# Second layer's weights assembled during the first layer and parked in DRAM as float32

## The chip, the cores and the metric

The kernel runs on one NeuronCore of one Trainium2 chip. What counts is the device time of one launch in microseconds: median 1091.19 us of three runs (1089.95 to 1091.54). The profile shows one execution by itself; its own time was 1087.0 us.

## The reference, cut to what matters

Two attentions over the same q, k, v (4 batches, 8 heads, 576 positions, 64 wide), one on averages of four positions and one over the nearest seven positions, are added and reshaped to 2304 rows of 512. Two dense layers follow:

```python
h = x @ w_in                                   # 2304x512 @ 512x2048
g = np.where(h > 0, h, np.exp(np.minimum(h, 0)) - 1)
x = g @ w_out                                  # 2048 -> 512
gate = x @ w_gate                              # 512 -> 1536
val  = x @ w_val
out  = (gate / (1 + np.exp(-gate)) * val) @ w_o2   # 1536 -> 512, float32 out
```

The five weight matrices arrive as float64 (they are float32 draws times a float64 scalar). [...]

## The kernel before, in words

**Weights.** A weight "unit" is 128x1024 words of input (512 KB): two of the 128-wide blocks of the hidden dimension for a column matrix, one block of rows for an output matrix. The first layer has 32 units (16 "in", 16 "out"), the second 36 (12 each of "gate", "val", "o2"). `add_weights` makes a float32 unit from a raw one in four instructions: `size` (L339, ScalarE: a scaled copy of the high words), `words_a` (L343, VectorE: a shift), and `words_b` (L347 and L349, VectorE: sign bit, then the three top bits of the low word). `add_weight_split` then makes two fp32r parts from the float32 unit: a rounded copy (L275 on ScalarE or L277 on VectorE) and the remainder (L371, GpSimd: 128x512 subtract).

**Products.** A product of two split numbers is three matmuls (`products`, L659 to L661): high by high, high by low, low by high. The first layer goes over 8 chunks of 288 rows; chunk 0 uses whole float32 weights (L684, L689), the others the split ones. A step is one of the 16 hidden blocks f of a chunk: gemm1 (12 matmuls of 288 columns), Relu and Exp (L725, L733 ScalarE), a combination (L729 VectorE), a rounded copy `g` (L275 or L277), the remainder of g (L736 GpSimd), and gemm2 (12 matmuls). There are two banks for h, two buffers e and three buffers g. The second layer goes over 5 tiles of 512 rows (the last 256) with 12 steps of 36 matmuls each; sigmoid (L799), two multiplications (L802), a rounded copy (L804), a remainder (L805).

**Where weights live.** 33 places hold the split first-layer weights (32 used). A second-layer unit takes a place as soon as the last chunk has used its first-layer weight for the last time; three more places are in a pool of their own. So the split of the second layer's weights runs beside the last chunk of the first layer. This stretch, 16 steps long, is called **the change** below.

**What sets the order.** Every operation is a task with an engine, a modelled cost and a due time. `Work.run` plays the program through once when it is built, starts on each free engine the ready task with the lowest due time, and writes the instructions in that order. On the chip each engine goes through its list in order. Tasks of the first layer's chain have due times 14 earlier than their step. The attention of batches 1 to 3 is spread over the first layer's steps (`spans`).

**Memory in time.** Attention buffers are closed when the last rows are ready; `open_two` then opens the pools of raw weights, float32 units and x. The buffers of gated values (`y`, and every second `e`) are opened by `close_one`, after the first layer's last matmul and store; sigmoids of odd steps and all rounded copies of y wait for that.

Of the kernel before, what the change touches and what calls it, by code (L numbers as in the profile page):

```python
# [18 lines left out]
P = 128  # L19
# [208 lines left out]
def attention_moe_moe(ctx: ExitStack, tc: tile.TileContext, q, k, v, w_in, w_out, w_gate, w_val, w_o2, ident_in, mask_in, band_in, picks_in, out):  # L228
# [54 lines left out]

    work = Work()
    add = work.add
    w_slots = Places(lambda i: pools["w"].tile([P, 2, 512], F32R, tag=f"w{i}", name="w"), NW)
    w_slots.name = "w"

# [25 lines left out]


    BIAS = (1023 - 127) // 8
    wt, ww = {}, {}
    split_places = lambda: range(NW - 1, -1, -1)  # L320

    def load_w(key, t):
        kind, f = key
        if kind in ("in", "gate", "val"):
            src = {"in": w_in, "gate": w_gate, "val": w_val}[kind]
            nc.sync.dma_start(
                out=t.rearrange("p (k c) t -> p k (c t)", c=P),
                in_=src[:, 2 * f * P:2 * (f + 1) * P].rearrange("(k p) c -> p k c", p=P))
        else:
            src = {"out": w_out, "o2": w_o2}[kind]  # L330
            nc.sync.dma_start(out=t.rearrange("p c t -> p (c t)"), in_=src[f * P:(f + 1) * P, :])

    def pairs(t):
        return t.rearrange("p (c t) -> p c t", t=2)

    def add_weights(keys, dues, raws, whole, after=()):

        def size(w, r):
            nc.scalar.mul(w.t.bitcast(F32), r()[:, :, 1].bitcast(F32), 2.0 ** -BIAS)  # L339

        def words_a(w):
            t = w.t.bitcast(I32)
            nc.vector.tensor_scalar(out=t, in0=t, scalar1=3, scalar2=None, op0=ALU.logical_shift_left)  # L343

        def words_b(w, r):
            t = w.t.bitcast(I32)
            nc.vector.scalar_tensor_tensor(  # L347
                out=t, in0=r()[:, :, 1], scalar=-0x80000000, op0=ALU.bitwise_and, in1=t, op1=ALU.bitwise_or)
            nc.vector.scalar_tensor_tensor(  # L349
                out=t, in0=r()[:, :, 0], scalar=29, op0=ALU.logical_shift_right, in1=t, op1=ALU.bitwise_or)  # L350

        made = {}
        for n, key in enumerate(keys):
            due = dues[n]
            raw, w = raws(n), whole(n)
            room = [w.whole] if isinstance(w, Half) else []
            r = lambda raw=raw: pairs(raw.t.bitcast(I32).rearrange("p a b -> p (a b)"))
            add("sp", 0.5, due - 36.0, lambda key=key, r=r: load_w(key, r()), writes=[raw], nbytes=P * 4096, after=after)
            add("act", 0.69, due - 4, lambda w=w, r=r: size(w, r), reads=[raw, *room], writes=[w])
# [5 lines left out]
    def add_weight_split(key, due):  # L365

        u = ww[key]
        w = wt[key] = w_slots.new(split_places) if len(wt) < NW else w2_ring.new()
        add(COPIER, (0.6, 0.4), due - 2, lambda engine: copy(engine, w.t[:, 0], u.t.bitcast(F32)),
            reads=[u], writes=[w], second=0)  # L370
        add("pool", 1.3, due - 1, lambda: nc.gpsimd.tensor_tensor(  # L371
            out=w.t[:, 1], in0=u.t.bitcast(F32), in1=w.t[:, 0], op=ALU.subtract), reads=[u, w], writes=[w])


# [288 lines left out]
    def add_store(c, due, acc):  # L663
        x2d[c] = pools["dram"].tile([P, NP, T1], F32, tag=f"x2_{c}", name="x2d")
        stored[c] = []
        for i in range(NP):
            t = out_ring.new()
            add(COPIER, (0.5, 0.5), due - 1, lambda engine, c=c, i=i, t=t: copy(engine, t.t, acc[i].t[:, :T1]),
                reads=[acc[i]], writes=[t], second=0)
            stored[c].append(add("sp", 0.5, due, lambda c=c, i=i, t=t: nc.sync.dma_start(  # L670
                out=x2d[c][:, i], in_=t.t), reads=[t], nbytes=P * T1 * 4))

    def add_whole(f, due, acc, last):

        if f == 0:
            acc[0] = [bank(i) for i in range(NP)]
        h, e, g = bank(6, 7), e_ring.new(), g_ring.new()
        wi, wo, x = ww["in", f], ww["out", f], xt[0]
        ge = lambda: g.t[:, 0].bitcast(F32)

        def gemm1():
            begun.append(1)
            for i in range(NP):
# [9 lines left out]
        add_weight_split(("in", f), time1(NF1 + f))  # L693
# [5 lines left out]
        add_weight_split(("out", f), time1(NF1 + f + 1))  # L699
        if f == NF1 - 1:  # L700
            add_store(0, due, acc[0])

    def add_first():
        made = []
        acc, last = {}, {}
        for s, (c, f) in enumerate(order):
            due = time1(s)
            if c == 0:
                add_whole(f, due, acc, last)
                continue  # L710
            if f == 0:
                acc[c] = [bank(i) for i in range(NP)]
# [37 lines left out]

    x2r_ring = ring("f2", "x2r", [P, T2], 2, ordered=False)
    x2_ring = [ring("x" + "ab"[i], "x2", [P, 2, T2], 4, F32R) for i in range(2)]
    e2_ring = [ring("e2" + "ab"[i], "e2", [P, T2], 1) for i in range(2)]
    y_ring = ring("g2", "y", [P, 2, T2], 2, F32R)

    def add_second(opened, exps, first_done):
        x2t = {}
        for n, t0 in enumerate(range(0, N, T2)):
# [24 lines left out]
            for f in range(NF2):  # L783
# [3 lines left out]
                for kind, where in (("gate", (4, 5)), ("val", (6, 7))):  # L787
# [10 lines left out]
                e, y = e2_ring[f % 2].new(), y_ring.new()  # L798
# [5 lines left out]
                add("act", 0.6, due, lambda T=T, e=e, y=y: nc.scalar.copy(y.t[:, 0, :T], e.t[:, :T]), reads=[e], writes=[y], after=first_done)  # L804
# [20 lines left out]
    with tc.manual_schedule():  # L825
# [39 lines left out]
        for p in range(NP):  # L865
# [5 lines left out]
        words = add_weights(  # L871
            w1, w1_due, lambda n: w_slots.new(lambda: range(NW - 1, U1 - 1, -1)), lambda n: Half(whole[n // 2], n % 2))
# [25 lines left out]

        def close_one():
            one.close()  # L900
            for name in ("xb", "g2", "e2b"):
                open_pool(ctx, name, reuse_waits="tile")

        closed = [add("none", 0, 0, close_one, after=made)]
        r_ring = ring("r2", "r", [P, 512, 2], 3, I32)
        u_ring = ring("r2", "u", [P, 512], 3)
        w2_ring = ring("w2", "w", [P, 2, 512], len(w2) - NW, F32R)
        w2_due = [time2(f + (kind == "o2")) - 38.0 for kind, f in w2]
        add_weights(
            w2, w2_due, lambda n: r_ring.new(), lambda n: u_ring.new(), after=opened)  # L910
        wt.clear()
        for n, key in enumerate(w2):
            add_weight_split(key, w2_due[n])
        add_second(opened, exps, closed)
        work.run()

# [44 lines left out]
```

## Time and profile before

| | |
|---|---|
| median of 3 runs | 1091.19 us |
| profiled execution | 1087.0 us (span 1085.2 us) |
| TensorE busy | 1007.7 us of the span |
| VectorE / ScalarE / GpSimd busy | 553.4 / 396.9 / 326.1 us |
| mean granted TensorE clock | 0.959 |

The page cuts the span in 40 slices of 27 us. TensorE is at 9 tenths nearly throughout; the dips are in the first three slices (loading, attention of batch 0) and in slices 21 to 24 (543 to 651 us), where VectorE is at 8 to 9 tenths and the clock row falls to 8. Before that VectorE stands at 3 to 6 tenths, after it at 2.

Times in the trace are from the start of the span. A busy TensorE counts a matmul until its modelled end, so its rate is read from the distance between two starts.

### The profile page before, as it was taken

To read this page: it belongs to the slowest core of one execution; us is meant where nothing else is said; L and a number is where in the kernel's file an instruction comes from. 1 tells how busy PE (TensorE), PEld (TensorE's weight loads), DVE (VectorE), ACT (ScalarE), POOL (GpSimd) and SP (SyncE) were. 2 spreads that over 40 slices of the span, in tenths; PEclk is the share of its full clock that TensorE was granted. 3 is DMA by queue.
4 is the path that set the end of the run, shared out by engine and by line. 5 is a ranking of instruction groups with operands and counts; after the bars stand their busy time and mean duration, and the time that the engine had idled before them with its cause. 6 is when DMAs were issued, how large, how long until landed. Compare 5 with 4: busy or idle time off the path is not lost.

```text
span 1085.2 us, 18891 instructions
## 1 busy us (share of the span) xinstructions
PE 1007.7 (93%) x7540; PEld 878.3 (81%) x7540; DVE 553.4 (51%) x1003; ACT 396.9 (37%) x939; POOL 326.1 (30%) x355
## 2 busy tenths in 40 slices
PE   7669889999999999998987559999999999999998
PEld 5547679999999999998976548888888888888897
DVE  5899996553646446453389992222222222322232
ACT  4654555543554445453444442112112111211121
POOL 4473873452235222363466641001001000100000
PEclk8569999999999999999988989999999999999999
DMA  9958332131402111032055541002000100100010
GB/s 165 304 166 235 68 73 54 34 84 28 94 26 68 33 45 50 12 114 84 20 158 156 156 139 39 1 0 78 1 1 22 47 1 1 49 1 1 1 39 20
DMA packets 111335, 72.28 MB, mean 67 GB/s; under 512 B 71440, under 2 KB 105360, under 8 KB 111248
## 3 DMA queue, kind: packets, MB, share of 16 engines
q1 hardware_dynamic: 111104, 70.82, 24.0%
q8 instruction: 59, 0.97, 0.4%
q14 instruction: 28, 0.23, 0.1%
q10 hardware_dynamic: 144, 0.26, 0.1%
HBM read 61.62 MB, written 9.44 MB: 65 GB/s over the span
## 4 chain that ended last, share of the span: by engine, by line
PE 77%; DVE 11%; issue 4%; DMA 3%; POOL 2%; SPq 2%; ACT 1%; DVEq 0%; POOLq 0%; ACTq 0%
PE bank L659 24%; PE bank L661 23%; PE bank L660 23%; DVE u L347 3%; PE bank L526 1%; DVE u L349 1%; DVE u L343 1%; SPq L409 1%; DVE w L347 1%; PE bank L684 1%; DVE w L343 1%; PE bank L445 1%; DMA w<-in_v_dram 1%; POOL w L371 1%; PE bank L566 1%
## 5 line engine op out<-in xcount | busy, mean ns | idle before, releaser
L659 PE MATMUL bank<-x,w 128*128 128x288 f32 (+2 forms) x928 | 318.5, 343 | 23.4 <-DVE e L729 22.5
L660 PE MATMUL bank<-x,w 128*128 128x288 f32 (+2 forms) x928 | 312.4, 337 | 0.8 <-POOL x L647 0.8
L661 PE MATMUL bank<-x,w 128*128 128x288 f32 (+2 forms) x928 | 311.8, 336 | 0.0
L659 PEld LDWEIGHTS bank<-x,w 128*128 128x128 f32 x928 | 175.8, 189 | 46.1 <-DVE e L729 25.9
L802 DVE TENSOR_TENSOR e<-bank,e 128x512 f32<-128x512 f32 (+1 forms) x120 | 76.4, 637 | 251.2 <-ACT e L799 173.6
L660 PEld LDWEIGHTS bank<-x,w 128*128 128x128 f32 x928 | 176.8, 191 | 17.7 <-POOL x L647 1.1
L661 PEld LDWEIGHTS bank<-x,w 128*128 128x128 f32 x928 | 176.8, 191 | 16.2
L736 POOL TENSOR_TENSOR g<-e,g 128x288 fp32r<-128x288 f32 x112 | 97.6, 872 | 188.2 <-ACT g L275 147.6
L660 PE MATMUL bank<-g,w 128*128 128x288 f32 x448 | 134.6, 300 | 5.5 <-POOL g L736 5.5
L659 PE MATMUL bank<-g,w 128*128 128x288 f32 x448 | 136.7, 305 | 0.0
L661 PE MATMUL bank<-g,w 128*128 128x288 f32 x448 | 133.4, 298 | 0.0
L779 POOL TENSOR_TENSOR x<-x2r,x 128x512 fp32r<-128x512 f32 (+1 forms) x20 | 24.1, 1221 | 270.6 <-ACT x L778 270.6
L799 ACT ACTIVATE e<-bank 128x512 f32<-128x512 f32 (+1 forms) x60 | 33.4, 556 | 187.4 <-PE bank L661 186.4
L729 DVE SCALAR_TENSOR_TENSOR e<-e,bank 128x288 f32<-128x288 f32 x112 | 50.2, 448 | 100.8 <-ACT e L733 94.1
L659 PE MATMUL bank<-w,y 128*128 128x512 f32 x216 | 85.5, 396 | 10.3 <-ACT y L804 10.3
L660 PEld LDWEIGHTS bank<-g,w 128*128 128x128 f32 x448 | 86.3, 193 | 6.9 <-POOL g L736 6.8
L725 ACT ACTIVATE e<-bank 128x288 f32<-128x288 f32 x112 | 46.1, 412 | 119.7 <-PE bank L661 104.3
L804 ACT CAST y<-e 128x512 fp32r<-128x512 f32 (+1 forms) x60 | 34.7, 578 | 150.7 <-DVE e L802 133.3
L659 PEld LDWEIGHTS bank<-g,w 128*128 128x128 f32 x448 | 86.1, 192 | 2.8 <-issue 1.9
L661 PEld LDWEIGHTS bank<-g,w 128*128 128x128 f32 x448 | 86.2, 192 | 0.0
L661 PE MATMUL bank<-w,y 128*128 128x512 f32 x216 | 85.1, 394 | 0.2 <-DVE y L805 0.2
L660 PE MATMUL bank<-w,y 128*128 128x512 f32 x216 | 85.0, 394 | 0.0
(115 smaller groups left out, 1428.6 us busy)
## 6 DMA issues: line engine op xcount, KB each, us to landing
w<-in_moe_w_in_dram SPq DMA_DIRECT2D x16, 512.0 KB
w<-in_moe_w_out_dram SPq DMA_DIRECT2D x16, 512.0 KB
r<-in_moe_w_gate_dram SPq DMA_DIRECT2D x12, 512.0 KB
r<-in_moe_w_val_dram SPq DMA_DIRECT2D x12, 512.0 KB
r<-in_moe_w_out_dram SPq DMA_DIRECT2D x12, 512.0 KB
x2d<-o SPq DMA_DIRECT2D x32, 144.0 KB
out_dram<-x2r SPq DMA_DIRECT2D x17, 256.0 KB
vrows<-in_v_dram SPq DMA_DIRECT2D x66, 64.0 KB
```

The source lines that it names most:

```text
L343: nc.vector.tensor_scalar(out=t, in0=t, scalar1=3, scalar2=None, op0=ALU.logical_shift_left)
L347: nc.vector.scalar_tensor_tensor(out=t, in0=r()[:, :, 1], scalar=-0x80000000, op0=ALU.bitwise_and, in1=t, op1=ALU.bitwise_or)
L659: nc.tensor.matmul(ps, sh, mh, start=first, stop=False)
L660: nc.tensor.matmul(ps, sh, ml, start=False, stop=False)
L661: nc.tensor.matmul(ps, sl, mh, start=False, stop=last)
L725: nc.scalar.activation(e.t, h.t[:, :T1], AF.Relu, scale=-1.0)
L729: nc.vector.scalar_tensor_tensor(out=e.t, in0=e.t, scalar=-1.0, op0=ALU.add, in1=h.t[:, :T1], op1=ALU.max)
L736: add("pool", 0.82, due - URGENT, lambda e=e, g=g: nc.gpsimd.tensor_tensor(out=g.t[:, 1], in0=e.t, in1=g.t[:, 0], op=ALU.subtract), reads= ...
L779: add("pool", 1.3, due, lambda T=T, raw=raw, x=x: nc.gpsimd.tensor_tensor(out=x.t[:, 1, :T], in0=raw.t[:, :T], in1=x.t[:, 0, :T], op=ALU.s ...
L799: add("act", 0.6, due, lambda T=T, e=e, gate=gate: nc.scalar.activation(e.t[:, :T], gate.t[:, :T], AF.Sigmoid), reads=[gate], writes=[e], ...
L802: add("dve", 0.64, due, lambda T=T, e=e, x=x: nc.vector.tensor_tensor(out=e.t[:, :T], in0=x.t[:, :T], in1=e.t[:, :T], op=ALU.mult), reads= ...
L804: add("act", 0.6, due, lambda T=T, e=e, y=y: nc.scalar.copy(y.t[:, 0, :T], e.t[:, :T]), reads=[e], writes=[y], after=first_done)
```

## The change

Second-layer units are no longer assembled at the change. During chunks 1 to 6 each unit is loaded in two halves (128x512 words, 256 KB), assembled by the same four instructions on 256 columns, and the float32 half (128 KB) is stored to a DRAM tile. Two raw halves share the one spare weight place, two assembled halves a new tile `mid`. The first raw load waits for the last split of first-layer weights. At the change a unit is then loaded as float32 (256 KB, three buffers u) and only split. The first three units take the places of the extra pool, formerly the last three did. Also: pool of y and both e buffers are opened in `open_two`; sigmoids wait for the first layer's last Exp and rounded copies of y for nothing more; the attention of batches 2 and 3 is due 1 to 4 steps earlier; the last chunk's stores go through the five f buffers.

```diff
-    def add_weights(keys, dues, raws, whole, after=()):
...
+    def add_words(due, raw, u, reads=()):
...
+        part = 0.5 if isinstance(raw.room, Places) and raw.room is not w_raws else 1.0
+        add("act", 0.69 * part, due - 4, size, reads=[raw, *reads], writes=[u])
+        add("dve", 0.6 * part, due - 3, words_a, reads=[u], writes=[u])
+        return add("dve", 1.8 * part, due - 2.5, words_b, reads=[raw, u], writes=[u])
...
-            add("dve", 0.5, due - 3, lambda w=w: words_a(w), reads=[w], writes=[w])
-            made[key] = add("dve", 1.5, due - 2.5, lambda w=w, r=r: words_b(w, r), reads=[raw, w], writes=[w])
...
+    def add_weights_away(keys, dues, after):
+
+        spare = w_slots.new(lambda: range(NW))
+        raws = Places(lambda i: pairs(spare.t[:, i].bitcast(I32)), 2)
+        halves = Places(lambda i: mid[:, i], 2)
...
+            for i in range(2):
+                due = dues(2 * n + i)
+                raw, u = raws.new(lambda: range(2)), halves.new(lambda: range(2))
...
+                    nc.sync.dma_start(out=away[key][:, i * 256:(i + 1) * 256], in_=u.t)
...
+                add("sp", 0.5, due - 16.0, lambda key=key, raw=raw, i=i: load_w(key, raw.t, i), reads=[spare], writes=[raw],
+                    nbytes=P * 2048, after=after)
+                add_words(due, raw, u, [spare])
+                kept[key].append(add("sp", 0.5, due, store, reads=[u], nbytes=P * 1024))
...
-    e2_ring = [ring("e2" + "ab"[i], "e2", [P, T2], 1) for i in range(2)]
+    e2_ring = ring("e2", "e2", [P, T2], 2)
...
-                    reads=[gate], writes=[e], after=first_done if f % 2 else exps)
+                    reads=[gate], writes=[e], after=exps)
...
+        def w2_away(m):
+            return time1(2 * NF1) + (time1(6.9 * NF1) - time1(2 * NF1)) * m / (2 * len(w2))
...
-        spans = {1: (12, 24), 2: (42, 56), 3: (74, 88)}
+        spans = {1: (12, 24), 2: (41, 54), 3: (71, 84)}
...
-            for name in ("w2", "r2", "xa", "f2", "e2a"):
+            for name in ("w2", "r2", "xa", "f2", "e2", "g2"):
...
-        add_weights(
-            w2, w2_due, lambda n: r_ring.new(), lambda n: u_ring.new(), after=opened)
...
+            due = time2(f + (kind == "o2")) - 38.0
+            ww[key] = u = u_ring.new()
+            add("sp", 0.5, due - 8.0, lambda u=u, key=key: nc.sync.dma_start(out=u.t, in_=away[key]), writes=[u],
+                nbytes=P * 2048, after=[*opened, *kept[key]])
+            add_weight_split(key, due, w2_ring.new() if n < len(w2) - NW else w_slots.new(lambda: range(NW)))
```

The modelled VectorE cost of assembling a unit goes from 0.5 + 1.5 to twice 0.3 + 0.9, and the tasks' order is worked out anew. VectorE's list at the change (chunk 7) before: L729 is the first layer's step, the three lines on `u` assemble a second-layer unit, `w<-u` is a rounded copy.

```order
L729 SCALAR_TENSOR_TENSOR e<-e,bank 128x288
L343 TENSOR_SCALAR u<-u 128x512
L347 SCALAR_TENSOR_TENSOR u<-r,u 128x512
L349 SCALAR_TENSOR_TENSOR u<-r,u 128x512
L277 CAST w<-u 128x512
L343 TENSOR_SCALAR u<-u 128x512
L347 SCALAR_TENSOR_TENSOR u<-r,u 128x512
L349 SCALAR_TENSOR_TENSOR u<-r,u 128x512
L729 SCALAR_TENSOR_TENSOR e<-e,bank 128x288
```

The same place of VectorE's list now (L761 is what L729 was):

```order
L761 SCALAR_TENSOR_TENSOR e<-e,bank 128x288
L277 COPY o<-bank 128x288
L277 CAST w<-u 128x512
L761 SCALAR_TENSOR_TENSOR e<-e,bank 128x288
L277 CAST w<-u 128x512 x2
L761 SCALAR_TENSOR_TENSOR e<-e,bank 128x288
```

Six assembling instructions between two steps are gone; rounded copies stay.

VectorE's list in chunk 3, while attention of batch 2 is in progress, before (`qT`, `kT`, `sums`, `sm`, `st` belong to attention):

```order
L729 SCALAR_TENSOR_TENSOR e<-e,bank 128x288
L277 COPY kT<-bank 128x4x112
L456 TENSOR_REDUCE sums<-kT 128x4x24
L729 SCALAR_TENSOR_TENSOR e<-e,bank 128x288
L484 TENSOR_TENSOR sm<-bank,mask 128x128 x2
L489 TENSOR_REDUCE st<-sm 128x8
L492 TENSOR_TENSOR sm<-sm,st 128x256
L499 TENSOR_REDUCE st<-sm 128x8
L500 TENSOR_SCALAR st<-st 128x8
L501 RECIPROCAL st<-st 128x8
L729 SCALAR_TENSOR_TENSOR e<-e,bank 128x288
```

The same work in the list now (`mid` is half a second-layer unit; L513 was L484, L521 was L492):

```order
L761 SCALAR_TENSOR_TENSOR e<-e,bank 128x288
L277 COPY o<-bank 128x288
L277 COPY qT<-bank 128x4x96
L352 SCALAR_TENSOR_TENSOR mid<-w,mid 128x256
L354 SCALAR_TENSOR_TENSOR mid<-w,mid 128x256
L485 TENSOR_REDUCE sums<-kT 128x4x24
L485 TENSOR_REDUCE sums<-qT 128x4x24
L761 SCALAR_TENSOR_TENSOR e<-e,bank 128x288
L348 TENSOR_SCALAR mid<-mid 128x256
L352 SCALAR_TENSOR_TENSOR mid<-w,mid 128x256
L354 SCALAR_TENSOR_TENSOR mid<-w,mid 128x256
L513 TENSOR_TENSOR sm<-bank,mask 128x128 x2
```

About one half unit (three instructions) has come into each step of chunks 1 to 6.

SyncE's list in chunk 3 before (`rows` and `vrows` are attention loads):

```order
L409 DMA vrows<-in_v_dram 32x8x64 x4
L409 DMA rows<-in_q_dram 96x8x64
L409 DMA vrows<-in_v_dram 32x8x64 x4
L409 DMA rows<-in_k_dram 112x8x64
L409 DMA rows<-in_q_dram 96x8x64
```

SyncE's list there, now (`w` is the raw half, `wd<-mid` the store of the assembled one):

```order
L386 DMA wd<-mid 128x256
L438 DMA vrows<-in_v_dram 32x8x64 x4
L331 DMA w<-in_moe_w_gate_dram 128x2x256
L386 DMA wd<-mid 128x256
L331 DMA w<-in_moe_w_gate_dram 128x2x256
L386 DMA wd<-mid 128x256
L438 DMA rows<-in_k_dram 112x8x64
L438 DMA rows<-in_q_dram 96x8x64
```

A load and a store of a half unit now stand between the attention loads, about one pair per step.

## Rows read from the trace of the kernel before

**Rows 1.** Busy time in stretches from 470 us on; columns in the first line.

```profile
core 0: us, PE busy (x) PEld busy (x) DVE busy (x) ACT busy (x) POOL busy (x), PEclk, DMA share, GB/s
470.00:500.00 30.00, 25.62 (x179) 24.91 (x178) 16.13 (x24) 14.43 (x34) 17.38 (x17) 0.94 0.46 146
500.00:545.00 45.00, 44.85 (x329) 44.07 (x329) 15.16 (x26) 19.65 (x45) 18.88 (x19) 1.00 0.08 24
545.00:648.00 103.00, 68.77 (x387) 61.88 (x386) 95.62 (x117) 48.92 (x95) 61.40 (x46) 0.89 0.51 155
650.00:700.00 50.00, 50.00 (x212) 40.51 (x211) 14.52 (x20) 9.51 (x16) 5.15 (x4) 0.97 0.08 21
```

**Rows 2.** Waits of TensorE, 545 to 660 us: in total, times, longest.

```profile
PE bank L659 <- DVE e L729: 18.4, 10, 4.2
PE bank L659 <- ACT y L804: 10.3, 1, 10.3
PE bank L660 <- POOL g L736: 5.5, 5, 1.4
```

**Rows 3.** Assembling lines: durations min/median/max in ns, and groups (busy, mean | idle).

```profile
L343 DVE TENSOR_SCALAR u<-u x36: 411/420/1169, 481.9 to 643.6; 128x512 int32<-128x512 int32 x36
...
L347 DVE SCALAR_TENSOR_TENSOR u<-r,u x36: 679/694/1843, 482.5 to 644.1; 128x512 int32<-128x512 int32 x36
...
L349 DVE SCALAR_TENSOR_TENSOR u<-r,u x36: 691/1170/1674, 483.3 to 645.9; 128x512 int32<-128x512 int32 x36
...
L349 DVE SCALAR_TENSOR_TENSOR u<-r,u 128x512 int32<-128x512 int32 x36 | 42.8, 1189 | 1.2
L347 DVE SCALAR_TENSOR_TENSOR u<-r,u 128x512 int32<-128x512 int32 x36 | 40.3, 1120 | 1.0
...
L343 DVE TENSOR_SCALAR u<-u 128x512 int32<-128x512 int32 x36 | 21.1, 586 | 5.0 <-ACT u L339 5.0
```

**Rows 4.** Matmuls of 512 columns at the change, shapes apart; two more groups have 20.

```profile
L659 PE MATMUL bank<-x,w 128*128 128x512 f32 x20 | 8.1, 405 | 1.1 <-DVE e L729 1.1
```

**Rows 5.** Starts of matmuls: 512 and 288 columns at full clock, 288 after a wait.

```profile
505.28 0.40 PE L661 MATMUL bank<-x,w 128*128 128x512 f32 x1
505.52 0.39 PE L659 MATMUL bank<-x,w 128*128 128x512 f32 x1
...
508.54 0.29 PE L659 MATMUL bank<-x,w 128*128 128x288 f32 x1
...
509.59 0.29 PE L661 MATMUL bank<-x,w 128*128 128x288 f32 x1
...
561.98 0.44 PE L660 MATMUL bank<-x,w 128*128 128x288 f32 x1
562.22 0.44 PE L661 MATMUL bank<-x,w 128*128 128x288 f32 x1
```

**Rows 6.** GpSimd: remainder of a weight, and of g (durations min/median/max).

```profile
L371 POOL TENSOR_TENSOR w<-u,w x36: 1260/1414/1847, 485.6 to 647.3; 128x512 fp32r<-128x512 f32 x36
...
L736 POOL TENSOR_TENSOR g<-e,g x112: 791/806/1264, 157.2 to 629.4; 128x288 fp32r<-128x288 f32 x112
```

**Rows 7.** Timeline: issue of a 512 KB load and the ScalarE instruction that waits for it.

```profile
634.46 0.37 SPq L326 DMA_DIRECT2D r<-in_moe_w_val_dram  x1
...
638.68 0.66 ACT L339 ACTIVATE u<-r 128x512 f32<-128x512 f32 x1 [2.74 <-DMA r<-in_moe_w_val_dram]
640.63 0.62 ACT L275 CAST w<-u 128x512 fp32r<-128x512 f32 x1 [1.29 <-DVE u L349]
```

**Rows 8.** Busy time in chunks 1 to 6, and in three stretches of them.

```profile
155.00:470.00 315.00, 312.78 (x3416) 296.39 (x3414) 170.60 (x411) 152.93 (x432) 112.96 (x149) 1.00 0.21 51
215.00:230.00 15.00, 14.62 (x182) 14.05 (x182) 13.79 (x25) 7.78 (x19) 12.58 (x15) 1.00 0.54 119
240.00:290.00 50.00, 50.00 (x648) 48.05 (x647) 20.58 (x54) 22.34 (x55) 13.62 (x20) 1.00 0.18 39
335.00:350.00 15.00, 15.00 (x189) 14.13 (x188) 10.67 (x18) 7.79 (x18) 11.09 (x11) 1.00 0.37 86
```

**Rows 9.** Waits in chunks 1 to 6: in total, times, longest.

```profile
ACT g L275 <- PE bank L661: 30.6, 38, 1.7
...
PEld bank L659 <- DVE e L729: 0.6, 1, 0.6
```

More of the change, by code (lines that the diff above doesn't have):

```diff
@@ L285, in attention_moe_moe @@
     add = work.add
+    mid = pools["w"].tile([P, 2, 256], F32, tag="mid", name="mid")
     w_slots = Places(lambda i: pools["w"].tile([P, 2, 512], F32R, tag=f"w{i}", name="w"), NW)
     w_slots.name = "w"
+    w_raws = Places(lambda i: pairs(pools["w"].tile([P, 1024], I32, tag=f"w{i}", name="w")), NW)
+    w_raws.name, w_raws.users = "raw", w_slots.users
     begun = []
@@ L333, in pairs, with size, words_a @@
     def pairs(t):
         return t.rearrange("p (c t) -> p c t", t=2)
-    def add_weights(keys, dues, raws, whole, after=()):
[L338 to L342, printed above, removed]
+    def add_words(due, raw, u, reads=()):
+        def size():
+            nc.scalar.mul(u.t.bitcast(F32), raw.t[:, :, 1].bitcast(F32), 2.0 ** -BIAS)
+        def words_a():
+            t = u.t.bitcast(I32)
@@ L352, in add_weights @@
+        part = 0.5 if isinstance(raw.room, Places) and raw.room is not w_raws else 1.0
+        add("act", 0.69 * part, due - 4, size, reads=[raw, *reads], writes=[u])
+        add("dve", 0.6 * part, due - 3, words_a, reads=[u], writes=[u])
+        return add("dve", 1.8 * part, due - 2.5, words_b, reads=[raw, u], writes=[u])
+    def add_weights(keys, dues, whole):
         made = {}
         for n, key in enumerate(keys):
-            due = dues[n]
-            raw, w = raws(n), whole(n)
-            room = [w.whole] if isinstance(w, Half) else []
@@ L357, in add_weights @@
-            r = lambda raw=raw: pairs(raw.t.bitcast(I32).rearrange("p a b -> p (a b)"))
-            add("sp", 0.5, due - 36.0, lambda key=key, r=r: load_w(key, r()), writes=[raw], nbytes=P * 4096, after=after)
-            add("act", 0.69, due - 4, lambda w=w, r=r: size(w, r), reads=[raw, *room], writes=[w])
-            add("dve", 0.5, due - 3, lambda w=w: words_a(w), reads=[w], writes=[w])
-            made[key] = add("dve", 1.5, due - 2.5, lambda w=w, r=r: words_b(w, r), reads=[raw, w], writes=[w])
+            raw, w = w_raws.new(lambda: range(NW - 1, U1 - 1, -1)), whole(n)
@@ L362, in add_weights, with store @@
+            add("sp", 0.5, dues[n] - 36.0, lambda key=key, raw=raw: load_w(key, raw.t), writes=[raw], nbytes=P * 4096)
+            made[key] = add_words(dues[n], raw, w, [w.whole])
             ww[key] = w
         return made
-    def add_weight_split(key, due):
+    def add_weights_away(keys, dues, after):
+        spare = w_slots.new(lambda: range(NW))
+        raws = Places(lambda i: pairs(spare.t[:, i].bitcast(I32)), 2)
+        halves = Places(lambda i: mid[:, i], 2)
+        kept = {}
+        for n, key in enumerate(keys):
+            away[key] = pools["dram"].tile([P, 512], F32, tag=f"w_{n}", name="wd")
+            kept[key] = []
+            for i in range(2):
+                due = dues(2 * n + i)
+                raw, u = raws.new(lambda: range(2)), halves.new(lambda: range(2))
+                def store(key=key, i=i, u=u):
+                    nc.sync.dma_start(out=away[key][:, i * 256:(i + 1) * 256], in_=u.t)
[3 more added lines that the diff above has]
+                kept[key].append(add("sp", 0.5, due, store, reads=[u], nbytes=P * 1024))
+        return kept
@@ L367, in add_weight_split @@
+    def add_weight_split(key, due, w):
+        wt[key] = w
         u = ww[key]
-        w = wt[key] = w_slots.new(split_places) if len(wt) < NW else w2_ring.new()
         add(COPIER, (0.6, 0.4), due - 2, lambda engine: copy(engine, w.t[:, 0], u.t.bitcast(F32)),
             reads=[u], writes=[w], second=0)
-        add("pool", 1.3, due - 1, lambda: nc.gpsimd.tensor_tensor(
+        return add("pool", 1.3, due - 1, lambda: nc.gpsimd.tensor_tensor(
             out=w.t[:, 1], in0=u.t.bitcast(F32), in1=w.t[:, 0], op=ALU.subtract), reads=[u, w], writes=[w])
@@ L666, in add_store @@
         for i in range(NP):
-            t = out_ring.new()
-            add(COPIER, (0.5, 0.5), due - 1, lambda engine, c=c, i=i, t=t: copy(engine, t.t, acc[i].t[:, :T1]),
+            t = (out_ring if c < NC - 1 else xf_ring).new()
+            add(COPIER, (0.5, 0.5), due - 1, lambda engine, c=c, i=i, t=t: copy(engine, t.t[:, :T1], acc[i].t[:, :T1]),
                 reads=[acc[i]], writes=[t], second=0)
             stored[c].append(add("sp", 0.5, due, lambda c=c, i=i, t=t: nc.sync.dma_start(
-                out=x2d[c][:, i], in_=t.t), reads=[t], nbytes=P * T1 * 4))
+                out=x2d[c][:, i], in_=t.t[:, :T1]), reads=[t], nbytes=P * T1 * 4))
     def add_whole(f, due, acc, last):
@@ L708, in add_first @@
             if c == 0:
-                add_whole(f, due, acc, last)
+                split_last = add_whole(f, due, acc, last)
+                if f == NF1 - 1:
+                    kept.update(add_weights_away(w2, w2_away, split_last))
                 continue
@@ L803, in add_second @@
                         out=e.t[:, :T], in0=x.t[:, :T], in1=e.t[:, :T], op=ALU.mult), reads=[x, e], writes=[e])
-                add("act", 0.6, due, lambda T=T, e=e, y=y: nc.scalar.copy(y.t[:, 0, :T], e.t[:, :T]), reads=[e], writes=[y], after=first_done)
+                add("act", 0.6, due, lambda T=T, e=e, y=y: nc.scalar.copy(y.t[:, 0, :T], e.t[:, :T]), reads=[e], writes=[y])
                 add("dve", 0.64, due, lambda T=T, e=e, y=y: nc.vector.tensor_tensor(
@@ L870, in attention_moe_moe @@
         whole = [w_slots.new(lambda: range(U1)) for _ in range(NF1)]
-        words = add_weights(
-            w1, w1_due, lambda n: w_slots.new(lambda: range(NW - 1, U1 - 1, -1)), lambda n: Half(whole[n // 2], n % 2))
+        words = add_weights(w1, w1_due, lambda n: Half(whole[n // 2], n % 2))
+        kept = {}
+        def w2_away(m):
+            return time1(2 * NF1) + (time1(6.9 * NF1) - time1(2 * NF1)) * m / (2 * len(w2))
         made = []
```

41 lines of the change are left out of this document (20 added, 21 removed).

## The prediction, made before the changed kernel ran

> **What bounds the kernel now.** I first read the page's table of slices, then busy time by stretches over its dips, then TensorE's waits there, then the instructions of the engine that is waited for. The reader should see that the program is a TensorE program with one hole. From 500 to 545 us TensorE is busy 44.85 of 45 us at full clock; from 545 to 648 us it is busy 68.77 of 103 us at a mean granted clock of 0.89, while VectorE is busy 95.62 [rows 1]. The waits say for whom: 18.4 us in ten waits for L729, the first layer's step on VectorE, 5.5 us for GpSimd, and one wait of 10.3 us for the first rounded y [rows 2]. L729 is short; what stands in front of it in VectorE's list are six assembling instructions per step. One unit costs 0.586 + 1.120 + 1.189 = 2.90 us there [rows 3], two units 5.8 us, while a step of TensorE is 24 matmuls at 0.131 us (eight of them from 508.54 to 509.59) = 3.14 us [rows 5]. So the change runs at VectorE's pace.
>
> **What the hole is worth.** Between 545 and 648 us stand 387 matmuls [rows 1]: 60 of 512 columns [rows 4] at 0.235 us and, but for one, 326 of 288 columns at 0.131 us [rows 5], together 14.1 + 42.7 = 56.8 us. The stretch took 103 us, so 46.2 us are lost: 34.2 as idle time, the other 12 by a slow clock, since after a wait matmuls start 0.24 us apart instead of 0.13 [rows 5]. Of the two levels, 2.4 and 1.2 GHz, that is the lower, and it falls after idle time. The stretch 470 to 500 us holds the first units of the second layer: 179 matmuls at 0.131 us are 23.4 us of 30 [rows 1], 6 us lost. Together 52 us are there to be had.
>
> **What goes and what is late next.** All 36 assemblies leave the change, so L729 has only rounded copies in front of it. Next is GpSimd. Per step it makes two weight remainders and one of g: 2 x 1.414 + 0.806 = 3.63 us by the medians, 3.31 by the shortest [rows 6], against TensorE's 3.14. In TensorE's new list eleven steps of chunk 7 follow each other without a second-layer block between, so GpSimd overruns by 11 x 0.49 = 5.4 us. The floor is 0: three g buffers let the chain run ahead by up to two steps, more than 11 x 0.17. The ceiling comes from the loads: with three buffers u a unit goes through load, rounded copy and remainder. A raw load of 512 KB took 4.2 us from issue to use, the rounded copy 0.62 [rows 7]; half the bytes cost at most that, so a third of 4.2 + 0.62 + 1.41 = 2.1 us per unit, 4.2 per step, and 11 x 1.06 = 12 us. I take 5, near the medians, and 3 of the 6 us at 470 to 500, where four remainders of x and of the first units still stand between the steps on GpSimd. So 8 us stay, with bounds 0 and 18. The Trainium skill (DMA: Bandwidth & Descriptors, Anatomy of one DMA) gives about 2.0 us fixed plus bytes at 436 GB/s; that would be 2.6 us for 256 KB as an estimate, 1.5 us per unit, and the loads would then cost nothing. The row's 4.2 us for 512 KB is a little above its 3.2.
>
> The 10.3 us for the first y go too, and are in the 46: y no longer waits for the first layer's last store, and its chain starts at the last Exp. In TensorE's new list four blocks of twelve 512-column matmuls (11 us) and three gemm2 stand between there and the first product with y; if that cover were gone, the chain would be late by some 3 us at most.
>
> **What is added to chunks 1 to 6.** 72 half units: 72 loads, 72 ScalarE copies, 216 VectorE instructions, 72 stores. Alone, a full unit costs 0.41 + 0.68 + 0.69 = 1.78 us on VectorE; at the change 2.90 [rows 3], with GpSimd busy 61.40 of 103 us [rows 1]. The 1.12 us between are time beside GpSimd: the same line takes 0.68 or 1.84. In chunks 1 to 6 GpSimd is busy 112.96 of 315 us, 36% instead of 60 [rows 8], so I scale them to 0.67: 2.45 us per unit, 88 us. From above: each half waits as long as a whole does at the change, 1.78 + 2 x 1.12 = 4.0 us, 145 us. From below: 1.78, 64 us. VectorE is busy 170.6 of these 315 us [rows 8]; it comes to 259 (82%), at most 315.
>
> The Trainium skill (SBUF — State Buffer, Who interferes with whom) says that a VectorE instruction with two SBUF inputs and a GpSimd one that reads SBUF exclude each other, and that the second stands still for the first's whole length. The range 0.68 to 1.84 in L347 agrees. By that rule twice as many instructions meet twice as many such waits, which is the upper end, and it speaks against halves.
>
> Is that hidden? TensorE is busy 312.78 of 315 us [rows 8]. The chain is ahead: 38 times a rounded copy of g waited for TensorE to free a g, and TensorE's weight loads waited only 0.6 us once for L729 [rows 9]. A half unit in front of L729 delays it by 0.9 to 2 us, less than the lead of up to two steps (6.3 us). Only dense stretches overflow: 215 to 230 us VectorE stands at 13.79 of 15, 335 to 350 at 10.67 [rows 8]. Spreading 88 us evenly adds 28%, or 4.2 us to each: 3.0 us too much in the first, none in the second. With attention waits in TensorE's own list I take 7 us, bounds 0 and 25. ScalarE: 72 x 0.33 to 0.5 us on 152.93 of 315, hidden. SyncE: 144 issues of 0.37 us [rows 7] are 53 us; behind a store that waits for VectorE stand attention loads, which have a lead of several steps, so they are hidden; without the lead each would hold up attention by the few us of one half unit. DMA: the raw bytes that took a 0.51 share over 103 us for some 30 units [rows 1] come to 63 for 36, the stores to half of that, and the share rises from 0.21 to about 0.5; no queue is full. The earlier attention and the other placing of y and of the last stores add no instruction: nothing.
>
> **Sum.** Against the profiled execution: 1087.0 - 52 + 8 + 7 = 1050 us. The median of the runs shown is 4.2 us above it, so 1054 us.
>
> **Rivals.**
> - VectorE becomes the bound of chunks 1 to 6 (the page's rule on halves). For it: 92% in one stretch already; against it: 54% on the mean, and long stretches at 41% to refill the lead [rows 8]. With 145 us, 46% is added everywhere: 5.7 and 2.6 us too much in the two stretches shown, and no room left to catch up; 25 us instead of 7, 1072 us. Chance 0.2.
> - The change stays bound by its supply, now the u loads and GpSimd: 18 instead of 8 us, 1064 us. For it: GpSimd's 3.63 us against 3.14. Chance 0.1.
> - Slower. ScalarE's `size` of a half waits at the head of its list for a load that SyncE issues only behind a store that waits for VectorE; Relu and Exp queue behind. Two halves in flight turn over in 4.2 + 0.5 + 2.0 + 0.8 us, 3.75 per half or 270 us for 72, which fits in 315, so as a rule nothing stalls. But what each half cost TensorE would count 72 times: from (52 - 8) / 72 = 0.6 us on the kernel is slower, at 1.0 us it takes 1087 + 28 + 4 = 1119 us. Against it: the lead of two steps. Chance 0.05.
> - It gives back exactly what it wins (0.6 us a half), 1091 us. Chance 0.03.
>
> **How the numbers follow.** The forecast has 0.62. Its own range is 1044 to 1064. The low end of the whole range is both costs at 0: 1087 - 52 + 4 = 1039, say 1040; the high end is the first rival with the change's ceiling, 1087 - 52 + 18 + 25 + 4 = 1082, say 1080. Within 0.2% (2 us, what a measurement here can tell) I leave 0.03. Faster: 0.62 + 0.2 + 0.1 = 0.92; slower 0.05.
>
> **What would show it.** In the new profile: the dips in slices 20 to 24 gone and the clock at 9 there; TensorE's waits for L729's successor in chunk 7 under 5 us and its waits for GpSimd as the largest; no wait for y over 1 us. VectorE at 80 to 90% in chunks 1 to 6, its assembling instructions at 1.1 to 1.3 us per half; TensorE's waits there up by some 7 us. A gain under 30 us with VectorE above 95% there would mean the first rival; a chunk 7 above 4 us per step with SyncE waiting on GpSimd, the second; ScalarE idle before `size` with TensorE waiting behind, the third.

## The result, and the profile after

The changed kernel takes 1053.9 us (median of four runs, 1053.41 to 1057.0) beside 1090.78 for the kernel before: a ratio of 0.9668, 95% interval 0.9648 to 0.9688. The forecast was 1054. The execution that was profiled took 1057.0 us (span 1055.2, mean granted clock 0.969, before 0.959).

The page's slices of 26 us, for TensorE, VectorE, TensorE's granted clock and the DMA engines:

```profile
PE   7768979999999999999999999999999999999998
...
DVE  4899998886787877873123422222223222222232
...
PEclk7569989999999999999999999999999999999999
DMA  9966516455554476433114420011002000100010
```

From slice 7 on TensorE stands at 9 tenths (the last slice apart), and the dips of slices 21 to 24 are gone; the clock is at 9 from slice 7 on. VectorE is now at 6 to 8 tenths in slices 7 to 18, where it assembles the halves (makes float32 numbers out of the two 32-bit words of each float64), and at 1 to 4 at the change (slices 19 to 23). Busy time of the stretches of [rows 1] and [rows 8], columns as there:

```profile
core 0: us, PE busy (x) PEld busy (x) DVE busy (x) ACT busy (x) POOL busy (x), PEclk, DMA share, GB/s
155.00:470.00 315.00, 307.88 (x3409) 288.79 (x3408) 252.95 (x601) 176.34 (x508) 142.29 (x180) 1.00 0.53 140
470.00:500.00 30.00, 30.00 (x238) 29.36 (x238) 11.39 (x20) 13.97 (x33) 21.85 (x23) 1.00 0.29 83
545.00:648.00 103.00, 100.13 (x588) 89.06 (x587) 34.75 (x54) 39.09 (x79) 57.26 (x51) 1.00 0.35 99
```

In the third stretch 588 matmuls stand where 387 stood, at full clock; VectorE's busy time there fell from 95.62 to 34.75 us. Part of this is second-layer work that has moved up. TensorE's waits from 500 to 660 us (before, from 545 to 660 us: [rows 2]): in total, times, longest.

```profile
PE bank L688 <- DVE e L761: 2.8, 4, 1.5
PE bank L688 <- DVE o L277: 1.6, 1, 1.6
```

18.4 us for L729 have become 2.8 for its successor L761; the wait for y (10.3) and those for GpSimd (5.5) are gone. The price stands in chunks 1 to 6, first in TensorE's waits from 155 to 470 us (the same columns; the kernel before, then the changed one), then in the lines of the halves there (busy, mean ns | idle before):

```profile
PE bank L659 <- DVE e L729: 0.4, 1, 0.4
...
PE bank L688 <- DVE e L761: 5.5, 6, 1.8
```

```profile
L354 DVE SCALAR_TENSOR_TENSOR mid<-w,mid 128x256 int32<-128x256 int32 x72 | 44.3, 616 | 2.5
L352 DVE SCALAR_TENSOR_TENSOR mid<-w,mid 128x256 int32<-128x256 int32 x72 | 38.1, 529 | 0.8
...
L348 DVE TENSOR_SCALAR mid<-mid 128x256 int32<-128x256 int32 x72 | 27.2, 388 | 5.7 <-ACT mid L344 5.3
```

A half costs 0.388 + 0.529 + 0.616 = 1.53 us, a unit 3.07: two halves cost more than a whole unit did at the change (2.90, [rows 3]).

For where the time went I use starts of instructions in two executions of like start, the kernel before once more and the changed kernel once more (below), in us:

| stretch | before | after | difference |
|---|---|---|---|
| start to chunk 1's first step (VectorE's L729 / L761) | 159.1 | 159.5 | +0.4 |
| to chunk 6's first step | 321.0 | 325.3 | +4.3 |
| to chunk 7's first step | 56.4 | 54.3 | -2.1 |
| to chunk 7's last step | 92.9 | 60.1 | -32.8 |
| to the first product with y | 21.1 | 16.7 | -4.4 |
| to the end of the span | 437.7 | 436.3 | -1.4 |
| span | 1088.2 | 1052.2 | -36.0 |

A difference here is not yet a loss or a gain, since the planner moved work across the steps: in the third, fourth and fifth stretch TensorE starts 372, 422 and 48 matmuls before, 390, 396 and 86 after. What TensorE loses in each is worked out in the section on the prediction.

### The profile page after: what moved, and what is told of

Read it like the earlier page. It is cut to its first block, busy times and chain, and to the rows that moved or that the text cites. A ratio compares the mean times of both kernels' runs of the same rounds, so it can differ in the third digit from the quotient of the medians.

```text
span 1055.2 us, 19383 instructions
## 1 busy us (share of the span) xinstructions
PE 1003.8 (95%) x7540; PEld 869.6 (82%) x7540; DVE 547.3 (52%) x1088; ACT 395.6 (37%) x972; POOL 344.9 (33%) x390
## 5 line engine op out<-in xcount | busy, mean ns | idle before, releaser
L688 PEld LDWEIGHTS bank<-x,w 128*128 128x128 f32 x928 | 174.3, 188 | 32.7 <-DVE e L761 12.3
L689 PEld LDWEIGHTS bank<-x,w 128*128 128x128 f32 x928 | 174.9, 188 | 17.0 <-POOL x L676 0.3
L690 PEld LDWEIGHTS bank<-x,w 128*128 128x128 f32 x928 | 174.7, 188 | 16.8
L768 POOL TENSOR_TENSOR g<-e,g 128x288 fp32r<-128x288 f32 x112 | 94.0, 840 | 167.7 <-ACT g L275 117.0
L688 PE MATMUL bank<-g,w 128*128 128x288 f32 x448 | 134.9, 301 | 1.6 <-DVE o L277 1.6
L689 PE MATMUL bank<-g,w 128*128 128x288 f32 x448 | 132.2, 295 | 0.0
L690 PE MATMUL bank<-g,w 128*128 128x288 f32 x448 | 131.9, 294 | 0.0
L761 DVE SCALAR_TENSOR_TENSOR e<-e,bank 128x288 f32<-128x288 f32 x112 | 50.3, 449 | 76.0 <-ACT e L765 66.2
L688 PEld LDWEIGHTS bank<-g,w 128*128 128x128 f32 x448 | 84.1, 188 | 4.1 <-DVE o L277 1.9
L689 PEld LDWEIGHTS bank<-g,w 128*128 128x128 f32 x448 | 84.6, 189 | 0.2
L690 PEld LDWEIGHTS bank<-g,w 128*128 128x128 f32 x448 | 84.5, 189 | 0.0
```

Source lines behind the costliest of these rows:

```text
L688: nc.tensor.matmul(ps, sh, mh, start=first, stop=False)
L689: nc.tensor.matmul(ps, sh, ml, start=False, stop=False)
L690: nc.tensor.matmul(ps, sl, mh, start=False, stop=last)
L761: nc.vector.scalar_tensor_tensor(out=e.t, in0=e.t, scalar=-1.0, op0=ALU.add, in1=h.t[:, :T1], op1=ALU.max)
L768: add("pool", 0.82, due - URGENT, lambda e=e, g=g: nc.gpsimd.tensor_tensor(out=g.t[:, 1], in0=e.t, in1=g.t[:, 0], op=ALU.subtract), reads= ...
```

## The experiments

**Where the last 4 us of the sum come from.** The sum against the profiled execution was 1050, and 4.2 us were added for the median. The kernel before and the changed one were each run again, unchanged.

> The kernel before once more, for its trace alone. In its first trace chunk 1 began at 156.2 us; in five traces of changed kernels, with the old and the new order of chunk 0, it began at 159.1 to 162.4. If that is scatter of the start, this trace lies at 157 to 161 us; if the changed kernels are late there by something of their own, at 155 to 157.

> The changed kernel once more, for a second trace. In its first trace chunk 1 began 6 us later than in the kernel before (the first step of chunk 1 on VectorE at 162.4 instead of 156.2 us), although nothing of the second layer is loaded before that. If this comes from the new order of VectorE's list in chunk 0 (theory A), the second trace has it too: 160 to 164 us, and the median stays at 1053 to 1057 us. If it is scatter between executions (theory B), the step begins at 155 to 160 us this time and the execution is correspondingly shorter.

Measured: the kernel before 1089.98 us (a single run); the changed kernel 1053.87 (1053.52 to 1054.07), ratio 0.9675 [0.9661, 0.9689]. The first step of chunk 1 on VectorE, in the first profile of the kernel before and in its repeat:

```profile
156.23 0.46 DVE L729 SCALAR_TENSOR_TENSOR e<-e,bank 128x288 f32<-128x288 f32 x1
```

```profile
159.09 0.46 DVE L729 SCALAR_TENSOR_TENSOR e<-e,bank 128x288 f32<-128x288 f32 x1
```

The same instruction 2.9 us later, and the execution 3.0 us longer (1087.0, 1090.0). The changed kernel's two profiles show it at 162.4 and 159.5, in executions of 1057.0 and 1053.97 us. From that step to the first product with y lie 491.6 and 491.4 us in the two profiles of the kernel before, 456.5 and 456.4 in those of the changed one (457.2 in a third). So about 3 of the 4.2 us are scatter of the start, which the first trace had early. The prediction had added the 4.2 us as the distance of its profiled execution from the median, without asking where it came from.

**Does VectorE's assembling make the hole? (kernel before)** The kernel before without the 108 VectorE instructions that assemble second-layer weights; loads, `size`, copies and remainders stay.

```diff
+            away = key[0] in ("gate", "val", "o2")
-            add("dve", 0.5, due - 3, lambda w=w: words_a(w), reads=[w], writes=[w])
+            add("dve", 0.5, due - 3, (lambda: None) if away else lambda w=w: words_a(w), reads=[w], writes=[w])
...
```

> The kernel before, with the 108 VectorE instructions that assemble the second layer's units left out; raw loads of 512 KB, ScalarE copies, rounded copies, remainders and the order of everything else stay (so the second layer's weights are not the reference's). It prices the hole from the other side. My theory (VectorE's assembly is what bounds the change): steps of chunk 7 fall from 6.5 to 6.8 us to 3.5 to 4.5, and the median to 1040 to 1052 us. The rival that raw loads of 512 KB through three buffers, or GpSimd, would hold the change as long: steps stay above 5.5 us and the median above 1070 us.

Measured: 1047.38 us (1045.47 to 1048.22), 0.9611 [0.9596, 0.9626]. TensorE's waits, 545 to 660 us, and busy time:

```profile
PE bank L660 <- ACT y L805: 2.2, 1, 2.2
PE bank L660 <- DVE e L730: 2.0, 3, 1.1
PE bank L661 <- POOL g L737: 1.6, 3, 0.7
```

```profile
545.00:648.00 103.00, 97.05 (x538) 84.30 (x537) 26.02 (x43) 54.52 (x107) 55.26 (x48) 0.98 0.52 158
```

VectorE's instructions alone are worth 42 of the 1089.8 us of this comparison; steps of chunk 7 fall from 6.5 to 6.8 us to between 3.3 and 4.9. The wait for y falls from 10.3 to 2.2 although nothing about y was changed: in the kernel before, y's rounded copy (L804) stands in ScalarE's list behind a copy that waits for assembling:

```profile
646.63 0.62 ACT L275 CAST w<-u 128x512 fp32r<-128x512 f32 x1 [2.64 <-DVE u L349]
647.16 0.61 ACT L804 CAST y<-e 128x512 fp32r<-128x512 f32 x1
```

The hole was rightly named. The changed kernel ends 7 us above this run (1054.47 in the same comparison, below), in total about what the next experiment takes away.

**What do the halves cost in chunks 1 to 6?** The changed kernel without the 216 VectorE instructions of the halves, in the same planned order.

```diff
+        words_a, words_b = (assemble_a, assemble_b) if part == 1 else (lambda: None, lambda: None)
         add("dve", 0.6 * part, due - 3, words_a, reads=[u], writes=[u])
```

> The 216 VectorE instructions that assemble the half units are left out; loads, ScalarE copies, stores, and the order of everything else stay (the second layer's weights are therefore not the reference's). It prices the halves on VectorE. If my term is right (7 us of cost in chunks 1 to 6, most of it VectorE), the steps of chunks 1 to 6 run 4 to 8 us faster between step 16 and step 96 and the median is 1046 to 1050 us. If VectorE's work is hidden, as the few waits for it in the second trace of the changed kernel suggest, the median stays within 2 us of 1054, and the cost of chunks 1 to 6 lies in the new order or in the start.

Measured: 1047.95 us (1046.3 to 1050.07), 0.9626 [0.9607, 0.9645]. From chunk 1's first step to chunk 7's it takes 373.2 us, the changed kernel 379.6 and 380.4 in two profiles: the instructions cost 6 to 7 us, nearly all in chunks 1 to 5 (318.6 against 325.3 and 326.3 to chunk 6's first step). There the instructions stand, too: in the first profile from 169 to 468 us, while chunk 6's first step is at 487. Busy time there:

```profile
155.00:470.00 315.00, 312.64 (x3461) 294.76 (x3459) 160.44 (x389) 177.33 (x515) 134.89 (x185) 1.00 0.52 141
```

VectorE without halves is at 160.44 us where the kernel before had 170.6, and GpSimd at 134.89 instead of 112.96 [rows 8]: the planner, seeing VectorE dearer, gave some attention work to GpSimd. Loads and stores of the halves remain in this run (DMA share 0.52), and TensorE's 312.64 us equal the 312.78 of the kernel before: by that, ScalarE, SyncE and the queues cost next to nothing (by TensorE's losses, worked out as below, 37.4 against 35.7 us, so about 2).

**Is the early y worth anything?** Pools of y and every second e are opened late again, with the old waits.

```diff
...
-                    reads=[gate], writes=[e], after=exps)
+                    reads=[gate], writes=[e], after=first_done if f % 2 else exps)
...
-            for name in ("w2", "r2", "xa", "f2", "e2", "g2"):
+            for name in ("w2", "r2", "xa", "f2", "e2a"):
...
```

> The pools of y and of every second e are opened again after the first layer's end, with the waits of the kernel before; assembly stays in chunks 1 to 6. My theory (the gain is the assembly that left the change; the first y alone is worth what it then waits for): the first product with y waits some 3 to 6 us, the chain behind the last store, and the median is 1057 to 1061 us. The rival that the early y is what gives the gain: the wait is 10 us as before and more of the 37 us goes back, 1065 us or more.

Measured: 1052.63 us (1051.57 to 1054.12), 0.9665 [0.9651, 0.9679], against 0.9675 [0.9661, 0.9689] in the same comparison. TensorE's waits from 600 to 640 us:

```profile
PE bank L688 <- ACT y L836: 1.2, 1, 1.2
PE bank L690 <- DVE y L837: 0.7, 1, 0.7
```

Two waits, 1.9 us together, come back and the time doesn't; from chunk 1's first step to the end of the span it takes 892.9 us, in the changed kernel 892.7. The 1057 to 1061 us that I expected did not come: no gain from the early y can be shown.

**What holds chunk 7 at 3.9 us a step?** On TensorE its steps from 564 us on start 3.46, 3.84, 3.85, 3.44, 3.99, 3.44, 4.86 (with twelve matmuls more), 4.81 and 3.49 us apart; from 514 to 552 us it is 3.17 throughout. First suspicion, the loads of u: from issue to use of 256 KB by the chain of waits in the first profile (start, us, what):

```profile
588.46 2.63 POOL w L400 x2
...
591.10 3.27 DMA u<-wd
...
594.46 0.06 DVE w L277
...
595.28 0.45 DVE e L761
...
595.78 0.40 PE bank L688
```

A remainder frees u, the load takes 3.27 us, and the copy waits for it with L761 and TensorE behind. A fourth buffer takes that wait away:

```diff
-    u_ring = ring("r2", "u", [P, 512], 3)
+    u_ring = ring("r2", "u", [P, 512], 4)
```

> Four instead of three buffers u for the float32 units at the change. If the loop of load, copy and remainder over the buffers sets the pace of chunk 7 (3.9 us per step in the trace against 3.14 of TensorE), a step falls to GpSimd's 3.4 us and the median by 3 to 5 us, to 1049 to 1051 us. If GpSimd alone sets the pace, or steps are held up by the rounded copies, nothing changes beyond 1.5 us.

Measured: 1053.75 us (1053.07 to 1054.26), 0.9674 [0.9659, 0.9688]: nothing gained, against the expectation, and eight steps of 3.85 us each. VectorE's waits from 560 to 600 us, first in the changed kernel (second profile), then with four buffers:

```profile
DVE w L277 <- DMA u<-wd: 8.1, 4, 4.3
...
DVE w L277 <- PE bank L690: 1.6, 2, 1.4
```

```profile
DVE w L277 <- PE bank L690: 7.5, 11, 1.4
```

The waits for loads are gone and eleven waits for TensorE stand where two stood: the rounded copy now waits until TensorE has used a place for the last time. The timeline of one step (start, us, instruction, idle before it in brackets):

```profile
574.54 1.29 POOL L400 TENSOR_TENSOR w<-u,w 128x512 fp32r<-128x512 f32 x1 [0.36 <-DVE w L277]
574.75 1.36 DVE L277 CAST w<-u 128x512 fp32r<-128x512 f32 x1
...
576.73 1.30 POOL L400 TENSOR_TENSOR w<-u,w 128x512 fp32r<-128x512 f32 x1
576.76 1.55 DVE L277 CAST w<-u 128x512 fp32r<-128x512 f32 x1 [0.66 <-PE bank L690]
...
578.23 0.44 DVE L761 SCALAR_TENSOR_TENSOR e<-e,bank 128x288 f32<-128x288 f32 x1
...
578.73 0.40 PE L688 MATMUL bank<-x,w 128*128 128x288 f32 x1 [0.42 <-DVE e L761]
...
582.58 0.40 PE L688 MATMUL bank<-x,w 128*128 128x288 f32 x1 [0.40 <-DVE e L761]
```

A circle: the copy at 576.76 waits for TensorE's last use of a place, then takes 1.55 us beside GpSimd's remainder; L761 stands behind it; and TensorE's next gemm1 waits for L761, which must free one of the two banks of h. The period is 582.58 - 578.73 = 3.85 us.

**Cutting the circle, one way.** The planner gives a second-layer weight its place only 2 modelled us after the last use, so that the copy comes later in VectorE's list.

```diff
+        return Work.now - user.freed >= buf.lag
...
+            w.lag = 2.0
```

> The changed kernel, but the planner gives a second-layer weight a place only 2 us after its last use. With four buffers u every step of chunk 7 took 3.85 us, and its trace shows a circle: a rounded copy on VectorE waits for TensorE to free a place, the first layer's step stands behind it, and TensorE waits for that step before it may fill the next bank of h. If this circle holds chunk 7, copies no longer wait in the list, steps there fall from 3.9 us to 3.2 to 3.5, and the median falls by 3 to 5 us, to 1049 to 1052 us. If loads or the steps' own chain hold it, steps stay at 3.8 us or more and the median at 1053 to 1055 us. (There are also fewer remainders per step, eight of them left for after the last step; so a gain does not by itself tell the circle from GpSimd's load, only VectorE's waits for TensorE in the trace do.)

Measured: 1051.59 us (1049.87 to 1052.35, five runs), 0.9662 [0.9648, 0.9676]. VectorE's wait for the place from 560 to 600 us is gone; TensorE's waits from 545 to 610 us are:

```profile
PE bank L699 <- DVE e L772: 1.0, 3, 0.4
```

Steps are 3.33 to 3.85 us with one of 4.9; from chunk 7's first to last it takes 58.2 us instead of 60.1. With as many matmuls in this stretch, TensorE loses about 2 us less there (3.6 instead of 5.5, worked out as in the next section). The direction is as the circle has it, but the interval overlaps that of the changed kernel, remainders and copies lie otherwise too, and VectorE's waits for loads fell as well, from 8.1 to 2.8 us. The circle was read with four buffers; with three, the wait for a place was only 1.6 us. So what it costs the changed kernel isn't separated: partly confirmed.

**Cutting it another way.** Remainders of second-layer weights may go to either engine; in the trace 34 of 36 run on VectorE.

```diff
+        if key[0] in ("gate", "val", "o2"):
+            return add(EITHER, (0.75, 1.3), due - 1, lambda engine: two(engine).tensor_tensor(
+                out=w.t[:, 1], in0=u.t.bitcast(F32), in1=w.t[:, 0], op=ALU.subtract), reads=[u, w], writes=[w])
```

> The remainders of the second layer's weights may go to VectorE; the planner then puts 33 of 36 there. After a fourth buffer u changed nothing, GpSimd should set the pace of chunk 7 (3.4 us of work per step, 89% busy). If so, steps fall from 3.9 us (3.4 to 4.8) towards TensorE's 3.2, and the median falls by 4 to 7 us, to 1047 to 1050 us. If the rounded copies or loads set it, or VectorE takes GpSimd's place (2 x 0.64 to 1.3 us of remainders, 0.45 and up to two copies per step), the median stays within 2 us of 1054.

Measured: 1053.97 us (1052.78 to 1054.55), 0.9679 [0.9663, 0.9694]: no gain, where I expected 4 to 7 us. In chunk 7 steps are 3.5 us apart, and from its first to its last it takes 55.6 us instead of 60.1. A rounded copy with no remainder beside it:

```profile
579.90 0.43 DVE L277 CAST w<-u 128x512 fp32r<-128x512 f32 x1
```

But from chunk 1's first step to chunk 7's it takes 383.1 us instead of 379.6 to 380.4. This is moved work and not a loss: twelve second-layer matmuls of 512 columns, 2.8 us, now stand in chunk 6 (402 matmuls in 57.1 us instead of 390 in 54.3) and no longer in chunk 7 (384 instead of 396). Of the 4.5 us, then, some 1.8 are a gain (TensorE loses 3.7 us in chunk 7 instead of 5.5), too little for these medians to show.

**Another modelled cost.** The change also raised the modelled VectorE cost of whole first-layer units; here it is put back, with the halves as they are.

```diff
+        a, b = (0.6, 1.8) if part < 1 else (0.5, 1.5)
```

> The modelled VectorE cost of a whole first-layer unit is set back from 0.6 + 1.8 to 0.5 + 1.5; the half units keep theirs. VectorE's list in chunk 0 is then that of the kernel before. Theory A (the order in chunk 0 costs 6 us): the first step of chunk 1 at 155 to 158 us and the median 4 to 7 us below the changed kernel, 1047 to 1050 us. Theory B (scatter): no difference beyond 2 us, 1052 to 1056 us.

Measured: 1052.37 us (1049.09 to 1052.77), 0.9654 [0.9633, 0.9674]; chunk 1 begins at 159.1 us, as in the others. 1.5 us less, not shown by the times; in the trace, chunks 1 to 5 take 323.8 us instead of 325.1 to 326.3.

**Both together**, and then in a second comparison of five rounds, beside the changed kernel:

> Both: the old modelled cost in chunk 0 and remainders on VectorE; the version that should beat both kernels. If the first was worth 1.5 us and the second 4 to 7, 1046 to 1049 us; if neither is, 1052 to 1054.

> The version with the old modelled cost in chunk 0 and the remainders on VectorE again, with more rounds. Its first median was 1049.25 us, while its two parts alone gave 1052.4 and 1054.0. If the first was no accident, 1048 to 1051 us, and a ratio to the kernel before of 0.9625 to 0.965; if it was, 1052 to 1054.

> The changed kernel in the same rounds, to compare with: 1053 to 1055 us.

Measured: 1049.25 us (1046.66 to 1050.9), 0.9633 [0.9609, 0.9657]; then 1049.22 (1048.44 to 1050.65), 0.9629 [0.9616, 0.9643], beside the changed kernel's 1054.47 (1053.55 to 1055.6), 0.9679 [0.9665, 0.9693]. The intervals don't meet: this version beats both kernels, by 5 us and 40 us. Its two parts, each too small to show alone, add up in the traces: chunks 1 to 5 take 322.7 and 323.9 us, as with the old modelled cost alone, and TensorE loses 3.9 and 4.0 us in chunk 7, about as with the remainders on VectorE alone. Why the old modelled cost shortens chunks 1 to 5 isn't settled.

## Why the prediction was right, step by step

The loss of TensorE (distance between two starts, less the median distance of that pair of shapes, summed where it is above zero) in four stretches, before (second profile) and after (second profile), worked out from the starts in the traces: 155 to 470 us 35.7 and 43.4; 470 to 500 us 7.4 and 2.5; 500 to 545 us 0.7 and 0.2; 545 to 650 us 46.0 and 6.3. In the first stretch the level depends on how the shapes are grouped (21 to 36 us before), the difference less so (7.6 to 9.8).

- **The hole, 52 us.** Measured 7.4 + 0.7 + 46.0 = 54.1, and the run without VectorE's assembling shows its cause.
- **The residual, 8 us.** 2.5 + 0.2 + 6.3 = 9.0. The size was right and the step behind it was not, so the agreement is luck. "Next is GpSimd": of TensorE's waits in chunk 7 none is for GpSimd. Its remainders act through VectorE, whose rounded copy takes 1.36 to 1.55 us beside one instead of 0.43. The u loads, my upper bound, do delay the chain, but the fourth buffer only exchanged that wait for another. The price of a load that the prediction quotes from the Trainium skill (DMA: Bandwidth & Descriptors, Anatomy of one DMA) is given there for DMAs issued through GpSimd; these loads are issued by SyncE, and the one in the chain above took 3.27 us beside the estimate of 2.6. And "three g buffers let the chain run ahead by up to two steps" failed: the two banks of h bind first, since L761 must free one before the next gemm1 but one. So an instruction that stands before L761 in VectorE's list and waits for TensorE can hold TensorE itself.
- **Chunks 1 to 6, 7 us.** 43.4 - 35.7 = 7.7, and 6 to 7 in the run without the halves. In this, one half was mis-sized: 1.53 us, not 1.22. Durations of its three lines in the changed kernel's first profile (min/median/max in ns):

```profile
L348 DVE TENSOR_SCALAR mid<-mid x72: 242/286/1161, 169.3 to 465.7; 128x256 int32<-128x256 int32 x72
...
L352 DVE SCALAR_TENSOR_TENSOR mid<-w,mid x72: 372/422/1234, 169.6 to 467.6; 128x256 int32<-128x256 int32 x72
...
L354 DVE SCALAR_TENSOR_TENSOR mid<-w,mid x72: 424/427/1325, 170.1 to 468.1; 128x256 int32<-128x256 int32 x72
```

Where no GpSimd instruction runs beside them, the three take 0.28, 0.42 and 0.43 us on the mean, so two halves alone cost 2.25 us and a whole unit 1.78: half the columns save less than half the time, which the prediction did not count. The rest, 3.07 - 2.25 = 0.82 us per unit, is time beside GpSimd. I had scaled it by GpSimd's busy share to 0.67 at 36%; the share became 45% (142.29 of 315), which gives 0.84. So the scaling held. VectorE's busy share still came out at 80% (252.95 of 315) beside the forecast 82%, because attention work moved to GpSimd and records of neighbouring instructions overlap.
- **Do halves meet GpSimd twice as often?** The Trainium skill (SBUF — State Buffer, Who interferes with whom) lets a VectorE instruction with two SBUF inputs and a reading GpSimd one exclude each other for the whole length of the first. The longest L352 agrees: 1.23 us beside 0.42 alone, with GpSimd's remainders of g at 0.84 on the mean. Twice as many such waits, as the prediction drew from it, would be some 1.7 us per unit at 45%; 0.82 was measured.
- **SyncE, ScalarE, DMA: nothing.** About 2 us by the run without the halves' words. DMA share 0.53, forecast 0.5.
- **y.** The 10.3 us did go, but mostly because VectorE was free, not because y was moved.
- **The 4.2 us.** Right in size; some 3 of them are scatter of the start.

Of the signs named beforehand, the dips, the clock, the waits for L729's successor (2.8 us) and for y came as said; TensorE's waits for GpSimd as the largest, and 1.1 to 1.3 us per half, did not.

The rivals: without the halves' VectorE instructions chunks 1 to 6 are 6 to 7 us faster, not 25, so VectorE was not the bound there; the change lost 9 us and not 18, and a fourth buffer for the loads gained nothing; and no wait of TensorE for ScalarE's `size` appears.

## What to carry to other kernels

When work is moved off a full stretch, ask first what it costs where it goes, at the shape it has there: here a halved instruction took more than half of the whole one's time even alone (0.42 us for 256 columns, 0.69 for 512). After a bottleneck is gone, look in each engine's list for an instruction that waits for the bounding engine with that engine's own releaser queued behind it, and count the buffers between the two (here two banks of h, not three g) before trusting a lead. Compare executions by stretches from a fixed step to a fixed step, so that the scatter of the start doesn't enter the sum, and count the matmuls in each stretch, so that moved work isn't taken for a gain.

## What the runs showed of the hardware

- A rounded copy of 128x512 on VectorE takes 0.43 us alone and 1.36 to 1.55 us beside a GpSimd remainder of 1.29 us. In the timeline above one starts at 574.75, 0.21 us after the remainder, and ends at 576.11, 0.28 us after the remainder's end; the next starts 0.03 us after its remainder and again ends 0.28 us after it. That the end follows the remainder's end, whatever the start, is how a wait for the remainder looks, not a slower copy.
- From issue to use, one load of 256 KB took 3.27 us and one of 512 KB 4.2 [rows 7]: half the bytes saved 0.9 us.
- A `scalar_tensor_tensor` on int32 with no GpSimd instruction beside it takes 0.42 us for 128x256 (L352 in the changed kernel) and 0.69 for 128x512 (L347 before).
- Loading and attention of batch 0 end at 156.2 or 159.1 us in two executions of one kernel, and at 162.4, 159.5 or 160.3 in three of the other; from there to chunk 7 the same kernel repeats within 1 us (379.6 to 380.4 in the three).
